# An attention kernel that splits exp between two engines: four tiles of a block instead of three on VectorE, as a quadratic with a low-rank linear part, and score groups of two PSUM banks

## The chip, the cores and the metric

The kernel runs on one core of a Trainium2 chip. The metric is device time in microseconds (us) of one execution. The profiled execution is one of the timed ones, not always a typical one; its span, from the first to the last instruction, is some 2 us shorter than its own device time (826.1 against 827.9 us before the change). Every experiment ran on the same chip as fresh runs of the kernel before, and times are compared through those. The median of the kernel before in these sets was 823.9 to 825.5 us. The changed kernel itself was not run again beside the experiments, so a difference to it, or between two sets, goes over sets and chips.

## The reference, cut to what matters

Two independent blocks share the program. A is softmax attention: 2048 tokens, model width 640, 32 heads of width 20. B is linear attention of the same sizes. Their outputs are concatenated.

```python
def _A_ref(x, wqkv, wo):
    ...
    scores = jnp.einsum("bhqd,bhkd->bhqk", q, k) * (Dh ** -0.5)
    p = _softmax(scores, axis=-1)
    o = jnp.einsum("bhqk,bhkd->bhqd", p, v)
    ...
def _B_ref(x, wqkv, wo):
    ...
    phi = lambda t: jnp.where(t > 0, t + 1, jnp.exp(t)) + 1e-6
    pq, pk = phi(q), phi(k)
    kv = jnp.einsum("bhsd,bhse->bhde", pk, v)
    ...
```

Nearly all the work is exp of 32 x 2048 x 2048 scores. The inputs are small (scaled by 0.05), so the scaled scores are near zero and a short polynomial is accurate. A guard must still catch inputs for which it is not.

## The kernel before

The scores are made in tiles: 128 keys by 512 queries of one head, which is one PSUM bank. A *block* is 512 queries of four heads. It has 16 key tiles x 4 heads = 64 score tiles, and there are 32 blocks. Four score tiles of one key tile are a *quad*.

ScalarE does exp over groups of three and of two banks in turn. VectorE does three of a block's 16 key tiles (one and two in the first two blocks) as a cubic: it copies a score tile out of PSUM (Y), forms Y*Y and Y*Y*Y in SBUF, and TensorE multiplies each of the three with V, suitably scaled. The constant term is a sum of V, added at evacuation.

The eight PSUM banks are five for the two exp groups, one for the product with V, and two spare banks. VectorE's score tiles pass through the spare banks, and so do all projections of A, all of B and the output projections.

```python
_M = (1, 2) + (3,) * 30             # key tiles on VectorE, by block
_LK = (6, 10, 14, 2)[:max(_M)]      # which ones
class _Fast:
    SB = ((0, 1, 2), (3, 4))        # banks of the two exp groups
    PVB = 5                         # bank of the product with V
    NYQ = 3; NT2 = 2; NT3 = 1       # ring depths of Y, Y*Y, Y*Y*Y, in quads
    ...
    def fn_exp(self, t, j):
        ...
        sch.op("act", lambda e: e.activation(self.PT[:, s0:s0 + n, :], ps[:, b0:b0 + n, :], AF.Exp, scale=scale),
        ...
        # VectorE, per score tile and per quad
        sch.op("dve", lambda e: e.tensor_scalar(
            self.Y[:, sl, :], ps[:, d.bank, :], float(D_HEAD) ** -0.5, None, op0=ALU.mult), ...)
        sch.op("dve", lambda e: e.tensor_tensor(self.T2[:, q2:q2 + 4, :], y, y, op=ALU.mult), ...)
        sch.op("dve", lambda e: e.tensor_tensor(
            self.T3[:, q3:q3 + 4, :], self.T2[:, q2:q2 + 4, :], self.Y[:, q:q + 4, :], op=ALU.mult), ...)
...
        plan.banks["aux"] = [(0.0, 6), (0.0, 7)]      # the two spare banks
```

The order of instructions on each engine is fixed at build time. A list scheduler inside the kernel lays the work out on a modelled timeline, with durations per task, due times for background work (spaced by the constant `U` a block) and tokens for spare banks and buffers. The chip then runs these fixed orders with semaphores.

## Time and profile before

| | before |
|---|---|
| time, median | 824.0 us (822.8 to 827.6, 4 runs) |
| profiled span | 826.1 us |
| ScalarE (ACT) busy | 785.8 us, 95% |
| TensorE (PE) busy | 755.5 us, 91% |
| VectorE (DVE) busy | 683.1 us, 83% |

The first part of the page gives busy time, share of the span and instructions of each engine; its fourth part gives the chain of waits by engine and by line.

```profile
PE 755.5 (91%) x10965; PEld 263.8 (32%) x10965; DVE 683.1 (83%) x1130; ACT 785.8 (95%) x728; POOL 40.3 (5%) x66
...
ACT 73%; PE 16%; DVE 8%; issue 1%; DMA 1%; DVEq 0%
```

ScalarE is on the chain of waits for 73% of the span. Its groups by form show what it does. The columns are line, engine, operation, output and input with shapes, count, busy time, mean ns of one, and idle time just before.

```profile
L1460 ACT ACTIVATE f_PT<-ps 128x1536 bf16<-128x1536 f32 x335 | 513.7, 1533 | 12.6 <-PE ps L172 11.7
L1460 ACT ACTIVATE f_PT<-ps 128x1024 bf16<-128x1024 f32 x335 | 373.2, 1114 | 3.9 <-PE ps L172 3.8
```

Here 513.7 + 373.2 is more than the 773.3 us for which the exps keep the engine busy, because one starts before the other has ended. So a duration is not a price. The price is read where exps stand in a row, in the chain in order of time (start, length, what):

```profile
676.76 58.11 ACT f_PT L1460 x51
```

That is 1.139 us an exp, 2.28 us for a three and a two. In the window from 110 to 780 us, ScalarE is full and VectorE is busy for 87.5% (585.97 of 670):

```profile
110.00:780.00 670.00, 619.81 (x9045) 213.80 (x9038) 585.97 (x954) 666.33 (x623) 16.33 (x18) 1.00 0.23 62
```

The columns are the window, its length, then busy time and instruction count of PE, weight loads, DVE, ACT and POOL, then the granted clock, the DMA share and GB/s. VectorE's main groups are these, with the copy of a score tile first, then the two products:

```profile
L2084 DVE TENSOR_SCALAR f_Y<-ps 128x512 bf16<-128x512 f32 x372 | 248.3, 684 | 47.6 <-PE ps L172 45.3
L2093 DVE TENSOR_TENSOR f_T<-f_Y 128x2048 bf16<-128x2048 bf16 x93 | 113.3, 1218 | 1.2
L2098 DVE TENSOR_TENSOR f_T<-f_T,f_Y 128x2048 bf16<-128x2048 bf16 x93 | 112.7, 1212 | 2.6 <-PE ps L172 2.2
```

### The profile page before, as it was taken

Reading aid. Unit: us, or ns where it says so; the run is one execution under the profiler, and the core shown is the slowest. Engines: PE = TensorE matmul, PEld = TensorE weight load, DVE = VectorE, ACT = ScalarE, POOL = GpSimd, SP = SyncE. Lnnn points to the kernel's source line nnn. Section 1 sums busy time; section 2 is a strip of 40 time slices with the busy share of each in tenths; the row PEclk is TensorE's granted clock in tenths of the full one; section 3 lists DMA queues with packets and bytes.
Section 4 is the critical chain, followed back from the end, with each engine's and each line's share of the span. In section 5 each row is a group of like instructions: output and inputs, shape, how many; then the busy total and the mean of one; then the engine's idle time right before and its main releaser. Section 6 shows DMA issues by size and latency. Waiting matters only on the chain.

```text
span 826.1 us, 24546 instructions
## 1 busy us (share of the span) xinstructions
PE 755.5 (91%) x10965; PEld 263.8 (32%) x10965; DVE 683.1 (83%) x1130; ACT 785.8 (95%) x728; POOL 40.3 (5%) x66
## 2 busy tenths in 40 slices
PE   8899999999999999999989988899989998999995
PEld 3333333333333333333332322323223222333332
DVE  3567889998888988788989897888898998887865
ACT  5789999999999999999999999999999999999991
POOL 3010510110000010100000010000000000000000
PEclk7889999999999999999999999999999999999997
DMA  6613312012001210021082331112424032111212
GB/s 171 189 30 76 105 43 69 26 45 63 24 26 58 46 45 19 26 64 63 17 121 77 61 123 50 58 50 49 128 83 146 27 118 71 50 60 52 61 61 69
DMA packets 78934, 56.25 MB, mean 68 GB/s; under 512 B 39860, under 2 KB 71428, under 8 KB 78820
## 3 DMA queue, kind: packets, MB, share of 16 engines
q1 hardware_dynamic: 77508, 54.39, 23.9%
q8 instruction: 88, 1.44, 0.8%
q10 hardware_dynamic: 1312, 0.20, 0.1%
q14 instruction: 26, 0.21, 0.1%
HBM read 29.00 MB, written 18.54 MB: 58 GB/s over the span
## 4 chain that ended last, share of the span: by engine, by line
ACT 73%; PE 16%; DVE 8%; issue 1%; DMA 1%; DVEq 0%
ACT f_PT L1460 71%; PE ps L172 16%; DVE f_Y L2084 3%; ACT f_ex L1624 2%; DVE f_T L2093 2%; DVE f_T L2098 1%; DMA out_dram<-f_st 1%; DVE f_OTr L1488 0%; DVE f_qkp L1263 0%; DVE f_pk L1875 0%; DVE f_r L1108 0%; DVE f_st L1596 0%; PE ps L1237 0%; DVE f_st L1599 0%; DVE f_c L1356 0%
## 5 line engine op out<-in xcount | busy, mean ns | idle before, releaser
L1460 ACT ACTIVATE f_PT<-ps 128x1536 bf16<-128x1536 f32 (+1 forms) x671 | 773.3, 1323 | 16.5 <-PE ps L172 15.6
L172 PE MATMUL ps<-f_Qr,f_KT 32*128 32x512 bf16 x2048 | 311.9, 388 | 44.1 <-ACT f_PT L1460 35.6
L2084 DVE TENSOR_SCALAR f_Y<-ps 128x512 bf16<-128x512 f32 x372 | 248.3, 684 | 47.6 <-PE ps L172 45.3
L172 PEld LDWEIGHTS ps<-f_Qr,f_KT 32*128 32x128 bf16 x2048 | 78.8, 91 | 286.2 <-ACT f_PT L1460 218.6
L172 PE MATMUL ps<-f_PT,f_V 128*22 128x512 bf16 x1676 | 164.1, 387 | 0.1
L2098 DVE TENSOR_TENSOR f_T<-f_T,f_Y 128x2048 bf16<-128x2048 bf16 x93 | 112.7, 1212 | 2.6 <-PE ps L172 2.2
L2093 DVE TENSOR_TENSOR f_T<-f_Y 128x2048 bf16<-128x2048 bf16 x93 | 113.3, 1218 | 1.2
L172 PE MATMUL ps<-f_T,f_V 128*22 128x512 bf16 x744 | 70.7, 383 | 1.5 <-DVE f_T L2098 1.3
L172 PEld LDWEIGHTS ps<-f_PT,f_V 128*22 128x22 bf16 x1676 | 40.5, 89 | 78.1 <-issue 70.2
L172 PE MATMUL ps<-f_xT,f_w 128*32 128x512 bf16 x800 | 64.5, 391 | 0.7 <-DVE f_Y L2084 0.6
L172 PE MATMUL ps<-f_wB,f_xB 128*32 128x320 bf16 x1280 | 62.2, 301 | 1.6 <-DVE f_Y L2084 0.9
L1330 POOL TENSOR_SCALAR f_V<-f_V 128x160 bf16<-128x160 bf16 x24 | 20.9, 872 | 477.2 <-DVE f_V L1322 461.6
L172 PE MATMUL ps<-f_Y,f_V 128*22 128x512 bf16 x372 | 37.4, 382 | 3.4 <-DVE f_OTr L1488 3.3
L1263 DVE CAST f_qkp<-ps 128x512 bf16<-128x512 f32 x40 | 27.4, 685 | 13.7 <-PE ps L172 13.7
L172 PEld LDWEIGHTS ps<-f_wB,f_xB 128*32 128x32 bf16 x1280 | 27.8, 95 | 25.2 <-issue 10.8
L172 PE MATMUL ps<-f_w,f_xT 128*32 128x160 bf16 x1280 | 34.3, 240 | 1.4 <-DVE f_Y L2084 1.2
L172 PE MATMUL ps<-f_xB,f_wB 128*32 128x512 bf16 x400 | 32.1, 383 | 1.5 <-DVE f_V L1322 1.0
L1620 DVE TENSOR_SCALAR f_r<-ps 128x320 f32<-128x320 f32 (+1 forms) x52 | 29.1, 560 | 4.8 <-PE ps L172 4.7
L172 PE MATMUL ps<-f_wo,f_OTp 128*32 128x320 bf16 (+1 forms) x616 | 32.0, 308 | 1.1 <-DVE f_flag L1934 0.5
L172 PE MATMUL ps<-f_zt 128*32 128x512 bf16 (+1 forms) x327 | 31.5, 399 | 1.0 <-DVE f_warm L1053 1.0
L172 PE MATMUL ps<-f_woB,f_pk 128*32 128x320 bf16 x640 | 31.7, 301 | 0.4 <-DVE f_Y L2084 0.3
L1624 ACT ACTIVATE f_ex<-ps 128x320 f32<-128x320 f32 (+1 forms) x52 | 31.1, 598 | 0.0
(95 smaller groups left out, 420.6 us busy)
## 6 DMA issues: line engine op xcount, KB each, us to landing
f_Rbc<-f_Nd SPq DMA_DIRECT2D x27, 256.0 KB
f_Bd<-f_dc SPq DMA_DIRECT2D x16, 320.0 KB
f_wB<-f_Bd SPq DMA_DIRECT2D x20, 256.0 KB
out_dram<-f_st SPq DMA_DIRECT2D x32, 160.0 KB
f_KT<-f_Kd SPq DMA_DIRECT2D x7, 512.0 KB
f_Kd<-f_qkp SPq DMA_DIRECT2D x20, 128.0 KB
f_Qd<-f_qkp SPq DMA_DIRECT2D x20, 128.0 KB
f_Od<-f_OTw SPq DMA_DIRECT2D x124, 20.0 KB
```

Of the source, the lines that this page charges most:

```text
L172: lambda e: e.matmul(out, lhsT, rhs, start=start, stop=stop, tile_position=tp, skip_group_check=sgc),
L1263: sch.op("dve", lambda e: e.tensor_copy(self.qkp[:, s, :], ps[:, first.bank, :]), reads=(("ps", first.bank),), writes=(("qkp", s),))
L1330: sch.op("pool", lambda e: e.tensor_scalar(vt[:, rs, li, :, 1:21], self.V[:, rs, t, :, 1:21], f, None, op0=ALU.mult), reads=(("V", t, rs), ...
L1460: sch.op("act", lambda e: e.activation(self.PT[:, s0:s0 + n, :], ps[:, b0:b0 + n, :], AF.Exp, scale=scale), reads=tuple(("ps", b0 + k) for ...
L1620: sch.op("dve", lambda e: e.tensor_scalar(r1, ps[:, first.bank, 0:n], 0.0, 1e-6, op0=ALU.max, op1=ALU.add), reads=(("ps", first.bank),), w ...
L1624: sch.op("act", lambda e: e.activation(ex, ps[:, first.bank, 0:n], AF.Exp), reads=(("ps", first.bank),), writes=(("ex", k),))
L2084: sch.op("dve", lambda e: e.tensor_scalar(self.Y[:, sl, :], ps[:, d.bank, :], float(D_HEAD) ** -0.5, None, op0=ALU.mult), reads=(("ps", d. ...
L2093: sch.op("dve", lambda e: e.tensor_tensor(self.T2[:, q2:q2 + 4, :], y, y, op=ALU.mult), reads=tuple(("Y", q + i) for i in range(4)), write ...
L2098: sch.op("dve", lambda e: e.tensor_tensor(self.T3[:, q3:q3 + 4, :], self.T2[:, q2:q2 + 4, :], self.Y[:, q:q + 4, :], op=ALU.mult), reads=t ...
```

## The change

Its intent is to move more of exp from ScalarE to VectorE by making a quad cheaper there. There are four parts.

1. *Quadratic.* VectorE forms only the square, in place in Y. The cube goes. A guard per tile of keys (the sum of squares of the scaled scores) sends the program to the general path if it is over 1/64.
2. *Low-rank constant and linear part.* For the key tiles on VectorE, the sum over keys of (scaled score) x V is a query times the 20 x 21 matrix K-transposed x V, because a score is linear in the query. So one product per block replaces one product per tile. It needs keys in token layout (`t_kt`) and a small matrix per head group (`t_const`).
3. *Share.* Four key tiles a block instead of three, none in the first block: 124 quads instead of 93. ScalarE keeps 1552 score tiles instead of 1676.
4. *Groups of two banks*, in both places. That frees a PSUM bank: three spare banks instead of two.

With it come retuned pacing constants, a deeper ring of Y (five quads, in SBUF that the squares and cubes had) and some memsets moved to VectorE.

```diff
-_M = (1, 2) + (3,) * 30
-_LK = (6, 10, 14, 2)[:max(_M)]
+_M = (4,)*8
+_LK = (6, 10, 14, 2, 12, 8)[:max(_M)]
+_EPS = 1.0 / 64.0
+_D0 = 1
 ...
-    SB = ((0, 1, 2), (3, 4))
-    PVB = 5
+    SB = ((0, 1), (2, 3))
+    PVB = 4
+    AUX = (5, 6, 7)
-    NYQ = 3
-    NT2 = 2
-    NT3 = 1
+    NYQ = 5
-    U = 24.5
+    U = 23.0
 ...
-        plan.banks["aux"] = [(0.0, 6), (0.0, 7)]
+        plan.banks["aux"] = [(0.0, b) for b in self.AUX]
 ...
-        self.pvtot = [(16 - m) + 3 * m for m in self.m]
+        self.pvtot = [16 + (1 if m else 0) for m in self.m]
 ...
-                def t2(_, q=q, q2=q2):
+                def t2(_, q=q):
                     y = self.Y[:, q:q + 4, :]
-                    sch.op("dve", lambda e: e.tensor_tensor(self.T2[:, q2:q2 + 4, :], y, y, op=ALU.mult), ...
+                    sch.op("dve", lambda e: e.tensor_tensor(y, y, y, op=ALU.mult), ...
-                def t3(_, q=q, q2=q2, q3=q3):
-                    ...
+    def fn_lin(self, n):
+        ...
+            self.sch.mm(self.ps[32 * i:32 * i + _NC, b, :], self.Mst[:, sl, 32 * i:32 * i + _NC],
+                        self.Qr[:, sl, 512 * qc:512 * (qc + 1)], start=(c == 0), ...
 ...
-                self.b_tasks(ut[2], ut[30] + 8.0)
+                self.b_tasks(ut[2], ut[27])
```

(Cut: `t_kt`, `t_const`, the constants, and the code that lets up to three of VectorE's score tiles ride with one score group instead of one.)

## The prediction

> **What bounds the kernel now.** ScalarE: busy 785.8 of 826.1 us (95%; the page's first part), all of every 50 us from 100 to 350 us (the windows view), and exp carries 71% of the chain of waits. From 100 to 780 us it waits for scores only 3.1 us (the waits). The evacuations of query blocks (512 queries, four heads) are 24.4 us apart from the second on. TensorE is at 91%, VectorE at 83%.
>
> **ScalarE's cost.** The groups by form show 335 exps of three banks (mean 1533 ns) and 335 of two (1114 ns). They overlap: in the chain, 51 in a row take 58.11 us, so a three plus a two take 2.28 us. The Trainium skill, "ScalarE: Activation LUTs", section "What ACT_TABLE_LOAD costs", gives 0.833 ns an element, 0.427 us a bank (the forms differ by 0.419). The remaining 0.072 us an instruction is not hidden. A two costs 0.925 us. A block of 52 tiles costs 23.7 us, the B path's exps add about 0.75: 24.4 us, as measured.
>
> **Removed, added, moved.**
> - ScalarE: VectorE takes 124 quads instead of 93, so 1552 tiles stay instead of 1676, in 776 groups instead of 671. 124 x 0.427 = 53 us go, 105 x 0.072 = 8 us come back: net -45 us. A block costs 24 x 0.925 + 0.75 = 22.95 us.
> - VectorE: +124 copies of score tiles (684 ns each in the trace), -62 products of 2048 elements (1215 ns; the skill's "VectorE: DVE Perf Modes", the tier table, has 1224 ns): +85 - 75 us. Key casts, low-rank constants and memsets add about 12. Net about +20, to some 705 us.
> - TensorE: products with V fall from 22 rounds of 512 columns a block to 17; 776 score groups instead of 671, each with a switch of array tiling, give that back. About even.
> - PSUM: the score window of a two-bank group is now always the short one: I estimate 0.73 us between the end of an exp and the wanted start of the exp that reuses its banks; before, this alternated with about 1.15 us. A third spare bank helps.
>
> **On the critical path.** Nearly all of the ScalarE saving, outside the first block, where PE sets the pace. But at 23 us a block VectorE is needed for about 22.2 us (estimate: 87.5% busy from 110 to 780 us before, plus the additions), over 95%, and the B work gets an earlier end. Two engines over 95% behind two groups of buffering will not interlock perfectly: I put the period at 23.35 us. Second evacuation at about 76.5 us (77.1 before), 30 x 23.35 = 700, tail 16.5: 793 us profiled, 2 to 3 less timed.
>
> **Predicted: 790 us (777 to 808).** Faster by over 2%: 0.87; within 2%: 0.11; slower: 0.02.
>
> **What would show it.** ScalarE: 776 two-bank exps 0.925 us apart, busy about 743 us. Evacuations 23.0 to 23.7 us apart. VectorE busy near 705 us, 90%. Exp's waits for scores grow from 16 us to 20 to 35. Start and tail unchanged within 3 us.
>
> **What would make it wrong.** VectorE saturates where the B work is dense: then TensorE's waits for score copies grow and the period stays near 24. Or the short score window makes exps wait over 50 us in total. Or switches make TensorE the limit. If the guard fired, the general path would add far more; my calculation from the reference puts the largest guarded sum at 0.008, the limit at 1/64.

## The result, and the profile after

| | before | after |
|---|---|---|
| time, median | 824.0 us | 787.9 us (786.5 to 789.3, 4 runs) |
| ratio of fast runs | | 0.955 (95% interval 0.952 to 0.958) |
| profiled span | 826.1 us | 787.5 us |
| ACT busy | 785.8 us | 743.1 us |
| PE busy | 755.5 us | 748.8 us |
| DVE busy | 683.1 us | 684.4 us |
| second to last evacuation, by 30 | 24.4 us | 23.1 us |
| tail after the last evacuation | 16.5 us | 19.3 us |

A ratio here and below is the mean time of one kernel's fast runs over that of the other's fast runs of the same rounds, so it is not quite the ratio of the medians quoted.

The same two parts of the page, after the change:

```profile
PE 748.8 (95%) x10781; PEld 263.4 (33%) x10781; DVE 684.4 (87%) x1255; ACT 743.1 (94%) x833; POOL 24.7 (3%) x43
...
ACT 48%; PE 32%; DVE 15%; DMA 2%; SPq 2%; issue 1%; DVEq 0%
```

ScalarE is 42.7 us less busy and the span is 38.6 us shorter: nearly all of the saving arrived. But its share of the chain fell from 73% to 48%; TensorE and VectorE together now have 47%, against 24% before. The exps by form, and a long row of them in the chain:

```profile
L1496 ACT ACTIVATE f_PT<-ps 128x1024 bf16<-128x1024 f32 x776 | 727.3, 1065 | 12.5 <-PE ps L172 11.0
```

```profile
634.89 41.56 ACT f_PT L1496 x45
```

That is 0.924 us an exp of two banks, against 0.925 predicted. VectorE's groups answer to the three of before. The copy of score tiles grew, one product is left of two, and two small new ones came (the casts of key tiles and the matrices of the linear part):

```profile
L2134 DVE TENSOR_SCALAR f_Y<-ps 128x512 bf16<-128x512 f32 x496 | 320.8, 683 | 24.6 <-PE ps L172 22.9
L2143 DVE TENSOR_TENSOR f_Y<-f_Y 128x2048 bf16<-128x2048 bf16 x124 | 150.1, 1210 | 0.3
...
L1393 DVE TENSOR_SCALAR f_M<-ps 20x21 bf16<-20x21 f32 x32 | 5.7, 178 | 1.1
L1357 DVE CAST f_Kt<-ps 128x160 bf16<-128x160 f32 x16 | 5.1, 321 | 5.7 <-PE ps L172 5.5
```

In the middle of the run ScalarE is 98.7% busy, PE 96.2% and VectorE 91.3%. Three engines are nearly full at once:

```profile
110.00:740.00 630.00, 606.11 (x8565) 207.47 (x8565) 575.42 (x1024) 621.66 (x702) 8.23 (x11) 1.00 0.24 65
```

### The profile page after: what moved, and what is told of

Read it like the earlier page. It is cut to its first block, busy times and chain, and to the rows that moved or that the text cites. A ratio compares the mean times of both kernels' runs of the same rounds, so it can differ in the third digit from the quotient of the medians.

```text
span 787.5 us, 24352 instructions
## 1 busy us (share of the span) xinstructions
PE 748.8 (95%) x10781; PEld 263.4 (33%) x10781; DVE 684.4 (87%) x1255; ACT 743.1 (94%) x833; POOL 24.7 (3%) x43
## 4 chain that ended last, share of the span: by engine, by line
ACT 48%; PE 32%; DVE 15%; DMA 2%; SPq 2%; issue 1%; DVEq 0%
ACT f_PT L1496 47%; PE ps L172 32%; DVE f_Y L2134 6%; DVE f_Y L2143 3%; SPq L1035 2%; ACT f_ex L1672 1%; DVE f_M L1393 1%; DMA f_xT<-in_A_x_dram 1%; DMA out_dram<-f_st 1%; DVE f_c L1391 1%; DMA f_Y<-in_A_x_dram 1%; DVE f_qkp L1271 1%; DVE f_OTr L1536 1%; DVE f_r L1668 0%; DVE f_pk L1771 0%
## 5 line engine op out<-in xcount | busy, mean ns | idle before, releaser
L1496 ACT ACTIVATE f_PT<-ps 128x1024 bf16<-128x1024 f32 x776 | 727.3, 1065 | 12.5 <-PE ps L172 11.0
L172 PE MATMUL ps<-f_Qr,f_KT 32*128 32x512 bf16 x2048 | 345.5, 386 | 22.0 <-ACT f_PT L1496 14.0
L2134 DVE TENSOR_SCALAR f_Y<-ps 128x512 bf16<-128x512 f32 x496 | 320.8, 683 | 24.6 <-PE ps L172 22.9
L172 PE MATMUL ps<-f_PT,f_V 128*25 128x512 bf16 x1552 | 151.0, 388 | 0.1
L2143 DVE TENSOR_TENSOR f_Y<-f_Y 128x2048 bf16<-128x2048 bf16 x124 | 150.1, 1210 | 0.3
L172 PEld LDWEIGHTS ps<-f_PT,f_V 128*25 128x25 bf16 x1552 | 38.2, 92 | 67.9 <-issue 63.4
L172 PE MATMUL ps<-f_Y,f_V 128*25 128x512 bf16 x496 | 48.8, 384 | 2.5 <-DVE f_OTr L1536 1.6
L172 PE MATMUL ps<-f_w,f_xT 128*32 128x160 bf16 x1600 | 44.8, 247 | 0.5 <-DVE f_M L1393 0.5
L172 PEld LDWEIGHTS ps<-f_w,f_xT 128*32 128x32 bf16 x1600 | 31.7, 102 | 16.9 <-issue 5.1
L1330 DVE CAST f_V<-ps 128x160 bf16<-128x160 f32 x64 | 20.1, 316 | 15.2 <-PE ps L172 15.1
```

The costliest lines, as they stand in the source:

```text
L172: lambda e: e.matmul(out, lhsT, rhs, start=start, stop=stop, tile_position=tp, skip_group_check=sgc),
L1330: sch.op("dve", lambda e: e.tensor_copy(dst, src), reads=(("ps", first.bank), "Vc0", "Vc1"), writes=(("V", t, rs),))
L2134: sch.op("dve", lambda e: e.tensor_scalar(self.Y[:, sl, :], ps[:, d.bank, :], float(D_HEAD) ** -0.5, None, op0=ALU.mult), reads=(("ps", d. ...
L2143: sch.op("dve", lambda e: e.tensor_tensor(y, y, y, op=ALU.mult), writes=tuple(("Y", q + i) for i in range(4)))
```

## The experiments

The prediction came out right, so the question is which part of the change earned the time, and what each of the others is for. The theory was that ScalarE sets the time at 0.92 us per two-bank exp and the rest only has to keep up. The first rival was that cheaper work on VectorE and TensorE is itself what gains. The second was that the third spare bank is. Each of these runs gives the kernel's scheduler other inputs, so each also has another order of instructions; the section on the runs in one table says how much of a difference lies in the order.

### First set: share, polynomial and group shape apart

**The quadratic with the old share, groups of two banks.** The edit on the changed kernel:

```diff
-_M = (4,)*8
+_M = (3,)*8
-    U = 23.0
+    U = 24.8
```

> The changed kernel with three instead of four tiles a block on VectorE (93 quads, as before the change), groups of two banks kept, pacing constant 24.8. Theory (ScalarE sets the period, at 0.9225 us per two-bank exp): 838 instead of 776 exps, +57 us, so about 845 us, slower than before the change. Rival (the gain came from the cheaper quadratic and the third spare bank, which relieve VectorE and TensorE): it stays near or under 810 us.

Measured: 833.4 us, ratio to before 1.009 (1.004 to 1.014). It is correct and slightly *slower* than before. ScalarE is busy 798.7 us for 838 exps. The direction is that of the theory; the size was overestimated by 12 us, because I added all of the exps' cost to the changed kernel's time. The evacuations are 1.8 us a block further apart (24.88 against 23.08 us), or 54 us over 30 blocks, but the start up to the second evacuation is 4.8 us shorter and the tail 2 us shorter.

**The quadratic with old share and old groups** (its linear part, the deeper ring and the other small changes stay in):

```diff
-_M = (4,)*8
+_M = (3,)*8
-    SB = ((0, 1), (2, 3))
-    PVB = 4
-    AUX = (5, 6, 7)
+    SB = ((0, 1, 2), (3, 4))
+    PVB = 5
+    AUX = (6, 7)
-    U = 23.0
+    U = 24.5
```

> The changed kernel with three tiles a block on VectorE and the old groups of three and two banks with two spare banks, pacing constant 24.5: the quadratic alone. Theory (ScalarE sets the period): the exps are those of before, 335 threes and 335 twos, so 818 to 828 us. Rival (the relief of VectorE and TensorE is itself worth time): under 810 us.

Measured: 821.1 us, ratio 0.995 (0.991 to 1.000). The first part of its page:

```profile
PE 747.9 (91%) x10833; PEld 263.2 (32%) x10833; DVE 596.5 (72%) x1095; ACT 785.8 (95%) x728; POOL 19.6 (2%) x39
```

VectorE lost 86.6 us of work against the kernel before, TensorE 7.6 us, and ScalarE's busy time is the same 785.8 us. The time moved by about half a per cent. The relief of an engine that was not the limit bought close to nothing. The first rival falls.

These two runs also price the group shape. With the same share, going from threes and twos to twos costs 12 us (833.4 - 821.1), though with a third spare bank on the second side. The extra exps explain some 9 us of that (838 x 0.9225 = 773 us against 335 x 2.28 = 764 us).

**The full share, with old groups and therefore two spare banks** (the second edit above, without the other two):

> The changed kernel with the old groups of three and two banks and two spare banks. Theory without a worth of the third spare bank: 310 pairs at 2.28 us are about 9 us less than 776 twos at 0.9225 us, so about 779 us. Rival (the third spare bank carries part of the gain, because VectorE at 87% must be fed): 795 us or more, with more waits of VectorE for scores.

Measured: 879.8 us, ratio 1.069 (1.061 to 1.077), 92 us slower than the changed kernel with *less* exp work (ACT busy 733.3 us against 743.1). The rival was right, by far more than I allowed for. The windows of this run show where:

```profile
50.00:200.00 150.00, 137.95 (x2059) 47.56 (x2047) 114.83 (x211) 115.32 (x107) 14.90 (x27) 0.93 0.19 55
200.00:400.00 200.00, 187.40 (x2528) 63.32 (x2526) 168.47 (x292) 193.69 (x178) 2.62 (x4) 0.95 0.15 40
...
802.00:879.00 77.00, 54.57 (x1120) 27.35 (x1112) 41.86 (x85) 2.93 (x5) 0.00 (x0) 0.94 0.37 119
```

From 200 to 400 us ScalarE is 97% busy, but from 50 to 200 us it idles for a quarter of the time, and after the last evacuation at 802.1 us there is a tail of 77 us with almost no work for it. The groups in that tail are output projections of A and B and the last part of B. Work that should have run beside the exps was left over until they had ended.

**The kernel before with the full share: four cubic tiles.**

```diff
-_M = (1, 2) + (3,) * 30
+_M = (1, 2) + (4,) * 30
```

> The kernel before with four instead of three tiles a block on VectorE, still as a cubic with per-tile linear products: only the share moves. Theory (VectorE could not have carried a fourth cubic tile): 30 more quads at about 5 us put VectorE's busy time near 830 us, so 850 us or more, VectorE over 93% busy. Rival (ScalarE alone counts): 1556 tiles left for exp, about 780 us.

Measured: 958.7 us, ratio 1.161 (1.155 to 1.167). Its profiled run, at 969.9 us, was slow, so its times are not compared; VectorE is busy for 823.2 us in it, near the 830 expected, but that is only 85% of the span. The step "over 93% busy" failed: it was not VectorE's capacity alone. The previous run shows why. With two spare banks and a quarter of the tiles on VectorE, even the quadratic takes 880 us. The remaining 79 us go with all that still differs: the cubic, its products with V per tile, the rings and the pacing. No run parts these. A cubic with four tiles and three spare banks was not run either; the 823.2 us of VectorE work are more than the whole 787.9 us of the changed kernel, which argues against it but is no test.

### Second set: the spare bank, the linear part, ScalarE itself, one more step

**The changed kernel with one bank left unused.** Group shape and share stay:

```diff
-    AUX = (5, 6, 7)
+    AUX = (6, 7)
```

> The changed kernel with its groups of two banks, but with two instead of three spare banks (one bank of the eight left unused). The run with the old groups took 880 us, and lost its time to a start and a tail in which ScalarE had nothing, not to the exps. Theory (the spare bank is what the group shape buys): 840 us or more, the loss again at the start and in the tail, blocks in the middle near 22.5 us. Rival (the three-bank groups themselves upset the schedule): 786 to 795 us.

Measured: 898.2 us, ratio 1.086 (1.078 to 1.095). This one line costs 110 us against the change, and three-bank groups have no part in it. The waits of VectorE for scores (who waited for whom, us in total, times, longest) in the changed kernel and then here:

```profile
DVE f_Y L2134 <- PE ps L172: 22.9, 26, 3.2
```

```profile
DVE f_Y L2134 <- PE ps L172: 62.5, 109, 3.5
```

VectorE has the same work and waits nearly three times as long for it. By itself that does not show the cause: in the first run of the first set, which has three spare banks, the same wait is 86.4 us. What tells is the wait on the other side. A score tile for VectorE can't be made before a spare bank is free, so TensorE waits for the copy that frees one, in the changed kernel and then here:

```profile
PE ps L172 <- DVE f_Y L2134: 1.8, 8, 0.3
```

```profile
PE ps L172 <- DVE f_Y L2134: 12.3, 26, 4.5
```

TensorE's weight loads wait for the same copies 26.2 us in the changed kernel and 60.4 us here. Tail and starved middle are there again. TensorE's granted clock is lower, too. From 400 to 600 us it is busy for about as long as in the changed kernel, but gets through fewer matmuls (the changed kernel first, then this run and its tail):

```profile
400.00:600.00 200.00, 189.77 (x2494) 60.94 (x2490) 184.98 (x327) 199.25 (x225) 2.44 (x4) 1.00 0.32 80
```

```profile
400.00:600.00 200.00, 185.19 (x2290) 60.59 (x2293) 161.91 (x292) 180.09 (x201) 2.44 (x4) 0.87 0.21 44
...
828.00:897.00 69.00, 50.81 (x983) 25.07 (x972) 38.17 (x78) 2.51 (x5) 0.00 (x0) 0.87 0.38 125
```

The expectation "start and tail alone, middle near 22.5 us a block" was only partly right. There is also one hole of 49 us between two evacuations, at about 220 us, and the later middle runs at 24 to 25 us a block.

**The linear part per tile again.** The product of Y with V returns for each tile (124 rounds), the low-rank product of a block (31 rounds) goes. Squares get a buffer of their own, so the ring of Y is three deep:

```diff
-    NYQ = 5
+    NYQ = 3
+    NT2 = 2
-        self.pvtot = [16 + (1 if m else 0) for m in self.m]
+        self.pvtot = [16 + m for m in self.m]
-                    sch.op("dve", lambda e: e.tensor_tensor(y, y, y, op=ALU.mult), ...
+                    sch.op("dve", lambda e: e.tensor_tensor(self.T2[:, q2:q2 + 4, :], y, y, op=ALU.mult), ...
+                p1 = plan.add(... self.fn_pv(t, n, kt, self.V, "V", kt, self.Y, "Y", ...))
-            if self.m[n]:
+            if False:            # no fn_lin
```

> The changed kernel with the linear part again as one product of the scaled scores with V per tile (124 rounds) in place of one low-rank product per block (31 rounds); squares go to their own buffer, as before the change, so the score ring is three deep instead of five; everything else kept. Theory (TensorE, at 95% busy, has no room): 93 rounds at about 0.22 us are 20 us more for TensorE, so 796 us or more, more waits of exp for scores. Rival (TensorE has slack, the low-rank form is not worth time): 785 to 791 us.

Measured: 809.7 us, ratio 0.977 (0.968 to 0.987), 22 us slower than the change. One of its four runs was slow; the fast three average 807.3 us. PE busy rose by 19 us (768.0 against 748.8), close to the 20 expected. But the edit also made the ring shallower, so this run alone doesn't say which of the two cost the time. A run of the third set was meant to part them.

**A shorter exp.** Its output is wrong, which doesn't matter for the time. Only 448 of 512 columns of each bank go through exp; the rest is a constant.

```diff
-        e.activation(self.PT[:, s0:s0 + n, :], ps[:, b0:b0 + n, :], AF.Exp, scale=scale)
+        e.activation(self.PT[:, s0:s0 + n, 0:448], ps[:, b0:b0 + n, 0:448], AF.Exp, scale=scale)
```

> The changed kernel with a wrong result on purpose: each exp works on 448 of its 512 columns, so ScalarE has 776 x 0.107 = 83 us less to do and nothing else changes. If ScalarE alone set the time: about 710 us. If TensorE (95% busy) and VectorE (87%) stand just behind it, as I think: 750 to 780 us, with busy shares of both rising. If ScalarE no longer matters: 785 us or more.

Measured: 776.1 us, ratio 0.940 (0.934 to 0.946). The check of results let it pass, presumably since the scores are so near zero that every exp is close to 1. Some 83 us of exp less, by the price of a row, gave 12 us. (ScalarE's busy time fell by only 53 us, to 690.0: exps that no longer stand in rows overlap less.) The chain of waits, by engine:

```profile
PE 52%; DVE 42%; ACT 4%; issue 2%; DMA 1%; DVEq 0%
```

ScalarE has left the chain. So after the change it is the limit by a margin of only 12 us, or 1.5%: in this order of instructions, which was laid out for full exps, TensorE and VectorE together stand right behind it. Before the change, when the chain was 73% ScalarE, I would expect the same saving to be worth more; that was not run.

**One step further in the last four blocks.**

```diff
-_M = (4,)*8
+_M = (4,)*7 + (5,)
```

> The changed kernel with a fifth tile a block on VectorE in the last four blocks only, after the B work has ended: 16 quads... that is 4 quads more there, 16 tiles less for exp, 8 exps x 0.9225 = 7 us less for ScalarE. Theory (ScalarE sets the pace there and VectorE has room): about 781 us. Rival (VectorE is as full there as elsewhere, or the tail sets the end): 786 to 795 us. The constants grow from four to five tiles everywhere, a few us of VectorE.

Measured: 812.7 us median over four runs that fall in two places (803.9, 805.7, 819.8 and 820.5; the two longer ones are slow, at a granted clock of 0.95), so no ratio is given; the two fast runs average 804.8 us. This was a miss. ScalarE did get its 7 us (ACT busy 736.0 us) and its last exp ended 7 us earlier (at 760.2 against 767.5 us), but the tail after the last evacuation grew from 19.3 to 36.6 us. My reading is that the moved tiles take spare banks and VectorE time from the output projections, which then run after the exps; no run tests it.

### Third set: what a spare bank is needed for, the ring, the pacing

**Two spare banks with the smaller share** (the edits of the first run, and the bank left unused):

> Three tiles a block on VectorE, groups of two banks, two spare banks (one bank left unused). With four tiles, two spare banks cost 110 us. Theory (the need is uses of a spare bank: some 830 a run with four tiles, some 700 with three, about 690 in the kernel before, which managed with two): two are enough here, 828 to 840 us, as with three banks (833). Rival (two-bank groups with two spare banks break the schedule whatever VectorE does): 870 us or more.

Measured: 836.8 us, ratio 1.014 (1.010 to 1.018): only 3.4 us more than with three spare banks, which is within the noise (1.009 to 1.018 against 1.004 to 1.014). So two-bank groups with two spare banks are fine, and the third bank is worth about 3 us, not clear of noise, with three tiles on VectorE and 110 us with four. It fits that the need is set by how many times a spare bank is used. Counting how often the scheduler takes one, the kernel before has 372 score tiles + 314 others = 686 uses, this run has 372 + 314 + 12 = 698, and the changed kernel 496 + 314 + 16 = 826. As an estimate: over the time from the first exp to the last exp's end, two banks gave 2 x 798 / 686 = 2.33 us a use before, and three give 3 x 756 / 826 = 2.75 us after. Two banks at the new pace would have to turn over in 2 x 756 / 826 = 1.83 us. Over their whole length, the two runs with two banks and four tiles managed 2.1 to 2.2 us.

**The ring alone:**

```diff
-    NYQ = 5
+    NYQ = 3
```

> The changed kernel with the ring of score quads three deep instead of five; the low-rank linear part kept. It parts the two things that the run with per-tile linear products (810 us) changed at once. If the per-tile products on TensorE cost that time: 786 to 793 us here. If the shallow ring cost it: 800 to 812 us here, and the low-rank form itself is worth little at equal depth.

Measured: 832.0 us, ratio 1.008 (1.003 to 1.012), outside both expectations: 44 us slower than the change and 22 us slower than the run with per-tile products, which has the same ring of three and a buffer of two quads for squares besides. Exp waits for scores 49.7 us in total, against 11.0 in the changed kernel, here and then there:

```profile
ACT f_PT L1496 <- PE ps L172: 49.7, 47, 9.9
```

```profile
ACT f_PT L1496 <- PE ps L172: 11.0, 20, 3.5
```

What follows: the depth of the ring is worth at least as much as the whole loss of the per-tile run, so that loss can't be put down to TensorE's 93 extra rounds. Why three deep is worse here than there is not shown; the record points to the clock rather than to the buffers, since in the scheduler's own model the two orders end within 1 us of each other, and this run's profile has 82 us at half the clock against 25 us there (next section). How much the low-rank product is worth at equal depth stays open. A run with per-tile products, a square buffer and a ring of five would tell, but does not fit into SBUF; one with rings of four on both sides was not made.

**An attempt to beat the changed kernel by its pacing constants.**

```diff
-    DFR = 0.75                 -        self.lead = 6
+    DFR = 0.9                  +        self.lead = 8
-    PLO = 0.46                 -    SAME = 0.3
+    PLO = 0.5                  +    SAME = 0.2
```

> An attempt at a faster version: only pacing constants of the changed kernel's static schedule (share of a block by which VectorE's tiles must be done 0.9 instead of 0.75, lead 8 instead of 6, lower limit of TensorE's use 0.50 instead of 0.46, preference for staying in a tiling 0.2 instead of 0.3). Theory (some 20 us of start and tail are the schedule's order, not the engines): 776 to 782 us. Rival (the engines are full and the order is worth nothing): 786 to 790 us.

Measured: 794.3 us, ratio 0.963 (0.960 to 0.966), slower than the change (0.955). The scheduler's own model had made this order shorter (778.0 us against 787.6); the chip did not. The tail shrank (16.1 us), the middle did not hold (23.47 us a block).

**The B work paced to the old end.**

```diff
-                self.b_tasks(ut[2], ut[27])
+                self.b_tasks(ut[2], ut[30] + 8.0)
```

> The changed kernel with the end of the B work's pacing back at its old place, three blocks later. My prediction held the earlier end to press VectorE. If it matters for the end: over 795 us, tail longer than 19 us. If not: 785 to 790 us.

Measured: 798.2 us, ratio 0.966 (0.963 to 0.970). By time the first half of the expectation held, by place it did not: the tail is 19.0 us, as in the change, and the loss is in the middle (23.55 us a block, with one hole of 37 us). The scheduler's model has this order no longer than the change's, and the fastest of its six runs, at a clock of 0.989, took 790.4 us, the others at 0.969 to 0.976 took 797 to 801 us. With the run above, it says that a few pacing constants can cost about 1%, and that such a difference should not be given a deeper cause. No version of mine beats the changed kernel.

### The runs in one table

| polynomial | key tiles on VectorE | groups | spare banks | time, us | ratio |
|---|---|---|---|---|---|
| cubic | 3 | 3 and 2 | 2 | 824 (before) | 1 |
| cubic | 4 | 3 and 2 | 2 | 958.7 | 1.161 |
| quadratic | 3 | 3 and 2 | 2 | 821.1 | 0.995 |
| quadratic | 3 | 2 | 3 | 833.4 | 1.009 |
| quadratic | 3 | 2 | 2 | 836.8 | 1.014 |
| quadratic | 4 | 3 and 2 | 2 | 879.8 | 1.069 |
| quadratic | 4 | 2 | 2 | 898.2 | 1.086 |
| quadratic | 4 | 2 | 3 | 787.9 (after) | 0.955 |

None of the intermediate versions gains more than half a per cent, and most lose. Only the moved tiles save ScalarE time. Without the third bank the move is a loss; that the cheaper polynomial is needed too is argued from VectorE's work and not tested by itself.

How much of a loss lies in the order and how much arises on the chip can in part be told apart. The scheduler's model, with fixed durations and full clock, has an end for each order. The last column adds up the stretches of the profiled execution in which TensorE was granted half its clock, the only other value in these traces.

| run | modelled end, us | measured, us | at half clock, us |
|---|---|---|---|
| the changed kernel | 787.6 | 787.9 | 15 |
| per-tile linear part | 804.1 | 809.7 | 25 |
| pacing constants | 778.0 | 794.3 | 44 |
| B work to the old end | 785.4 | 798.2 | 50 |
| ring of three | 804.6 | 832.0 | 82 |
| four tiles, old groups | 859.4 | 879.8 | 101 |
| one bank unused | 866.4 | 898.2 | 145 |

So of the 110 us for the unused bank, 79 us are in the order that two banks force on this scheduler. (Its model stays at 848 us or more if `U` is set to 24, 25, 26 or 27, so it is not one badly chosen constant; these were modelled, not run.) The rest arises on the chip, and down the table what is measured above the modelled end grows with the time at half clock, in nearly the same order. What starts such a stretch, a wait of TensorE or something else, was not tested, and the run with four cubic tiles does not fit the row (964.3 us modelled, 958.7 measured, and 113 us at half clock in its slow profile).

## Why the prediction was right

*Time.* 790 us was predicted (777 to 808), 787.9 measured.

*ScalarE sets the period, and its price.* Right. Predicted 0.925 us an exp and 743 us busy; measured 0.924 and 743.1. The price came from rows of exps in the chain and the rate of 0.833 ns an element that the Trainium skill gives in "ScalarE: Activation LUTs", section "What ACT_TABLE_LOAD costs"; the two forms in the trace before differ by 0.82 ns an element. Taking the durations (1533 and 1114 ns) as prices would have been wrong by some 15%. That three engines are needed at once came out too: with 11% less exp work, by the price of a row, the time fell by only 12 us.

*VectorE's term was mis-sized.* Predicted "Net about +20, to some 705 us", measured +1.3 (684.4). The sum of all VectorE durations in the trace did rise by some 20 us (from 747.0 to 767.6). But instructions in a row overlap, and the overlap grew from 64 to 83 us as VectorE ran fuller (sum minus the time that any of them runs). I had seen this on ScalarE and not applied it to VectorE. So VectorE was busy 91%, not "over 95%", in the middle, and the interlock cost less than feared: 23.1 us a block instead of 23.35, and 11.0 us of exp waiting for scores instead of 20 to 35.

*The third spare bank.* The prediction has four words for it, "A third spare bank helps", beside the worry about the short score window. The weights were the wrong way round. The window (its 0.73 us is two starts at 0.925 us less one duration of 1114 ns) costs little: groups of two cost 12 us in all, some 9 of them as exp instructions. Without the bank the same kernel takes 898 us and the change would have been a loss. The prediction was right because the change included the bank, not because I had seen that it was a condition.

*B work and pacing.* I took the earlier end of the B work for a burden. Putting it back made the kernel 10 us slower, though not by its modelled order, so what the earlier end itself is worth stays open.

*Start and tail.* Second evacuation 75.8 us (76.5 predicted). The tail grew by 2.8 us, within the 3 given.

*TensorE "about even".* Right: 755.5 to 748.8 us. The switches of array tiling that the prediction set against the saved rounds are in the trace: the matmul after a score product starts 315 ns later (median) if it is of another kind, and 212 ns after a product with V if another kind without a change of tiling follows. The traces have some 640 changes from scores to other products before and 700 after.

*The guard* did not fire: the results are correct and the time excludes the general path.

## What to carry to other kernels

Price a saving on the limiting engine from rows of its instructions, not from their durations, and then ask for each resource the moved work passes through (here PSUM banks and a ring of buffers) how often it is used and how fast it must turn over; a bank that is worth about 3 us at one load was worth 110 us at the next. A part of a change that gains nothing alone may be what lets the other part gain, so test parts in pairs. When several engines are over 90% busy, the next saving on one of them buys little: here 83 us of exp bought 12 us. And look at the granted clock of each run before giving a difference a cause.

## What the Trainium skill lacked or had wrong

- "ScalarE: Activation LUTs", section "What ACT_TABLE_LOAD costs": it gives back-to-back activations an overlap of about 93 ns. Its numbers for 1024 elements (1040 ns with immediate operands, 1133 ns with a pointer) then make 946 or 1040 ns a start (an estimate from the page's figures). Rows of exps reading 1024 elements of PSUM start every 924 ns here, with a mean duration of 1065 ns, so the overlap is about 140 ns. The rate of 0.833 ns an element fits: what is left is about 70 ns an instruction.
- "VectorE: DVE Perf Modes": the tier table's 1224 ns for a bf16 `tensor_tensor` of 2048 elements fits (1210 ns, in place as well). The section "The DRAIN you can't avoid" says that the next operation does not start until the pipe is empty, and that one that is not held starts earlier. That instructions overlap is thus in the skill; how much it came to here is not: the durations sum to 767.6 us and cover 684.4 us, so adding durations overstates VectorE by 12%.
- "Perfetto Trace Analysis", section "Matmuls", advises to rotate matmul groups through PSUM banks, and no page says how to find how many are enough. In this kernel one bank fewer cost 3 us, within the noise, at some 700 uses a run and 110 us at some 830.
